# Mean, variance and 1e-6 of the solu by scales of powers of two, and four one-column operations off the vector engine

## The chip, the cores and the metric

The kernel runs on one core of one Trainium2 chip. The metric is the device time of one execution in microseconds (us), lower is better. The core's engines, with the names that the profile uses, are TensorE (PE; PEld is its weight load), VectorE (DVE), ScalarE (ACT), GpSimd (POOL) and SyncE (SP, which here only issues transfers). Each works through its own queue in order, and they wait for each other by semaphores.

## The reference

Attention over chunks of 64 positions, then a feed-forward layer whose activation is a "solu" with a layer norm. The inputs are 8 batches, 8 heads, 576 positions and 64 columns a head, so 4608 tokens of 512 columns; the hidden layer has 1024 columns. The weights `w_in` and `w_out` come in 64-bit floats, the output is 32-bit.

```python
scores = scale * np.matmul(q_c, k_c.transpose(0, 1, 2, 4, 3))
scores = scores - np.max(scores, axis=-1, keepdims=True)
attn = np.exp(scores)
attn = attn / (np.sum(attn, axis=-1, keepdims=True) + 1e-09)
out = np.matmul(attn, v_c)
...
h = x @ w_in
e = np.exp(h - np.max(h, axis=-1, keepdims=True))
sm = e / (np.sum(e, axis=-1, keepdims=True) + 1e-09)
solu = h * sm
mu = np.mean(solu, axis=-1, keepdims=True)
var = np.mean((solu - mu) ** 2, axis=-1, keepdims=True)
ln = (solu - mu) / np.sqrt(var + 1e-06) * g_ln
return (ln @ w_out).astype(np.float32)
```

The division by the sum of exponentials cancels in the layer norm, up to 1e-6: with s that sum, the kernel leaves `h * e` undivided and adds 1e-6 times (s + 1e-9) squared to the variance.

## The kernel before

The 4608 tokens are 36 tiles of 128, numbered from 0. For each tile the kernel makes the scores and the softmax of two chunks (`sx` in PSUM, `s_e` or `e` beside it), turns the weights round into `attn_t`, multiplies with `v` into `x`, splits `x` into a high and a low part (`x_h`, `x_l`), and computes `ph = x @ w_in` as 24 products of 128x128 by 128x512: high times low, high times high, low times high. There is one `ph` buffer, so a tile's sums start only when the tile before has been read out of it. The solu follows, then the transposed `z` is split into `z_h` and `z_l`, and 24 products with `wo_h` and `wo_l` make `po`, in three thirds; `store` scales by `r` and writes out.

What the solu does to a tile, and on which engine:

- `solu_a`: VectorE takes the maximum of `ph` (`h_nmax`), ScalarE the exponential (`z`, with its row sum `h_sum`).
- `solu_b`: VectorE multiplies `ph` by it in place (`z`, row sum `z_sum`) and makes `nmean`, minus the mean, one column. Then the mean is subtracted, on GpSimd for tiles 0 to 4 and on ScalarE from tile 5 on.
- `solu_c`: VectorE adds 1e-9 to the sum (`ssum`), and makes 1e-6 times its square (`eps`), both one column.
- `variance`: ScalarE sums the squares (`sq`, `ssq`), VectorE makes `u = ssq / 1024 + eps`, one column, and GpSimd `r = u ** -0.5`.

The program has two parts. The opening is the table `START`: loads, the conversion of the 64-bit weights into a high and a low 32-bit part (16 pieces, `w_a`, `w_p2`, `w_r`, mostly VectorE and GpSimd), and the first five tiles. There a scheduler decides the order of the instructions on each engine, so that a removed instruction can move others. From tile 5 on (`order.on`) every engine keeps the order in which the loop at the end of the function issues.

GpSimd and SyncE share the transfers that finish the transposes: 8 of 16 for `z_t` and 4 of 8 for `attn_t` go out by each, every second tile.

Of the kernel before, what the change touches and what calls it, by code (L numbers as in the profile page):

```python
# [50 lines left out]
def chunk_attention_then_solu_ffn(  # L51
# [20 lines left out]
    NCC = DM // P  # L72
    NFC = FF // P
    SCALE = 1.0 / float(D) ** 0.5
    LO_DVE = (0, 6, 7, 10, 14)
    LO_TT = (0, 1, 3, 5, 6, 8)
    LO_POOL = (0, 1, 3, 4, 5)
# [10 lines left out]
    const = ctx.enter_context(tc.tile_pool(name="const", bufs=1))  # L88
    stage = ctx.enter_context(tc.tile_pool(name="stage", bufs=2))
    work = ctx.enter_context(tc.tile_pool(name="work", bufs=2))  # L90
    small = ctx.enter_context(tc.tile_pool(name="small", bufs=3))
# [5 lines left out]
    order = Order(tc)  # L97
    order.on = False
    pe, dve, act, pool, sync = (
        order.engine(e)  # L100
        for e in (nc.tensor, nc.vector, nc.scalar, nc.gpsimd, nc.sync)
    )
# [2 lines left out]
    make_identity(nc, ident)  # L105
    mhalf = const.tile([P, 1], F32, name="mhalf")
    nc.gpsimd.memset(mhalf, -0.5)
    g_sb = const.tile([P, NFC], F32, name="g_sb")
    ident_r = const.tile([P, P], F32R, name="ident_r")
    nc.vector.tensor_copy(out=ident_r, in_=ident)  # L110
# [2 lines left out]
        out=minus_r, in0=ident, scalar1=-1.0, scalar2=None, op0=ALU.mult  # L113
# [108 lines left out]
    def piece_rest(x):  # L222
# [30 lines left out]
        pe.matmul(ps, one_r, r, start=False, stop=True)  # L253
        if x in LO_DVE:
            dve.tensor_copy(out=d, in_=ps)
# [47 lines left out]
    def chunk_of(i, c):  # L303
        n = 2 * i + c
        return n // NCH, n % NCH

    def qk_turn(i):

        (b0, n0), (b1, n1) = chunk_of(i, 0), chunk_of(i, 1)
        if b0 == b1:  # L310
            parts = [(b0, n0, 0, 2)]
        else:
            parts = [(b0, n0, 0, 1), (b1, n1, 1, 2)]
        qk_tiles(i)
        for b, n, c0, c1 in parts:
            g = slice(2 * n, 2 * n + 2 * (c1 - c0))
            for to, of in ((QT, QS), (KT, KS)):
                dve.transpose(
                    out=to[i][:, :, c0 * CH:c1 * CH],
                    in_=of[b][:, :, g, :].rearrange("p a g d -> p a (g d)"),  # L320
                )
# [19 lines left out]
    def load_v(i):  # L341
        V[i] = work.tile([P, H, D], F32, name="v_sb", bufs=4)
        for p0, p1, b, s in tile_parts(i):
            sync.dma_start(
                V[i][p0:p1], v[b, :, s:s + p1 - p0, :].rearrange("h t d -> t h d")
            )
# [15 lines left out]
    st = {}  # L362
# [22 lines left out]
    def softmax_a(i):  # L385
# [12 lines left out]
        )  # L398
        act.activation(e, e, AF.Exp, scale=SCALE)
        st[i, "e"] = e  # L400
# [88 lines left out]
    def ffn_in(i):  # L489
        xh, xl = st[i, "x"]  # L490
        ph = st[i, "h"] = ps_h.tile([P, 2, HALF], F32, name="ph")

        sums = [(n, cc, m) for n in range(2) for cc in range(NCC) for m in range(3)]
        if i == 0:
            sums.sort(key=lambda s: s[1])
        else:

            sums.sort(key=lambda s: (s[0], s[2] == 2))
        for n, cc, m in sums:
            cols = slice(n * HALF, (n + 1) * HALF)  # L500
            x, w = ((xh, wi_l), (xh, wi_h), (xl, wi_h))[m]
            pe.matmul(
                ph[:, n, :], x[:, cc, :], w[:, cc, cols],
                start=(cc == 0 and m == 0), stop=(cc == NCC - 1 and m == 2),
            )
# [12 lines left out]
    def solu_b(i):  # L518
        ph = st.pop((i, "h")).rearrange("p n f -> p (n f)")
        z, esum = st.pop((i, "he"))  # L520
        zsum = small.tile([P, 1], F32, name="z_sum")
        dve.scalar_tensor_tensor(
            out=z, in0=ph, scalar=1.0, in1=z, op0=ALU.mult, op1=ALU.mult,
            accum_out=zsum,
        )
        nmean = small.tile([P, 1], F32, name="nmean")
        dve.tensor_scalar(
            out=nmean, in0=zsum, scalar1=-1.0 / FF, scalar2=None, op0=ALU.mult
        )
        if order.on:  # L530
            act.activation(z, z, AF.Identity, bias=nmean)
        else:
            pool.tensor_scalar(
                out=z, in0=z, scalar1=1.0, scalar2=nmean, op0=ALU.mult, op1=ALU.add
            )
        st[i, "z"] = z, esum
        if not order.on:
            solu_c(i)

    def solu_c(i):  # L540
        z, esum = st[i, "z"]

        ssum = small.tile([P, 1], F32, name="ssum")
        dve.tensor_scalar(
            out=ssum, in0=esum, scalar1=1e-9, scalar2=None, op0=ALU.add
        )
        eps = small.tile([P, 1], F32, name="eps")
        dve.scalar_tensor_tensor(
            out=eps, in0=ssum, scalar=1e-6, in1=ssum, op0=ALU.mult, op1=ALU.mult
        )  # L550
        st[i, "z"] = (z, eps)

    def variance(i):
        z, eps = st.pop((i, "z"))
        sq = work.tile([P, FF], mybir.dt.bfloat16, name="sq", bufs=1)
        ssq = small.tile([P, 1], F32, name="ssq")
        act.activation(sq, z, AF.Square, accum_out=ssq)
        u = small.tile([P, 1], F32, name="u")
        dve.scalar_tensor_tensor(
            out=u, in0=ssq, scalar=1.0 / FF, in1=eps, op0=ALU.mult, op1=ALU.add  # L560
        )
        r = small.tile([P, 1], F32, name="r", bufs=7)
        pool.tensor_tensor(out=r, in0=u, in1=mhalf, op=ALU.pow)
        st[i, "n"] = (z, r)
# [5 lines left out]
    def z_turn(i):  # L570
        z, _ = st[i, "n"]
        if i % 2 == 0:
            turned["b"] = work.tile([P, 4, 2, NFC, 32], F32, name="z_b", bufs=1)
        zb = turned["b"]
        dve.transpose(
            out=zb[:, :, i % 2, :, :].rearrange("p q a t -> p a q t"),
            in_=z.rearrange("p (a q c) -> p a q c", q=4, c=32),
        )
        alone = direct(i + 1)
        if i % 2 == 1 or alone:  # L580
            zt = work.tile([P, 4, 2, NFC, 32], F32, name="z_t")
            of = slice(0, 1 if alone else 2)
            for x in range(4):
                for y in range(4):
                    (pool if (x + y) % 2 else sync).dma_start(
                        zt[x * 32:(x + 1) * 32, y, of].rearrange("p s a t -> p (s a t)"),
                        zb[y * 32:(y + 1) * 32, x, of].rearrange("p s a t -> p (s a t)"),
                    )
            for m in (i,) if alone else (i - 1, i):
                st[m, "zr"] = zt  # L590
# [4 lines left out]
    def z_split(i, f):  # L595
        zt = st[i, "zr"][:, :, i % 2, :, :].rearrange("p y a t -> p a y t")
        zhv, zlv = (x.rearrange("p a (y t) -> p a y t", t=32) for x in (ZH, ZL))
        act.copy(zhv[:, f], zt[:, f])
        dve.tensor_tensor(
            out=zlv[:, f], in0=zt[:, f], in1=zhv[:, f].bitcast(F32), op=ALU.subtract  # L600
        )
# [59 lines left out]

    def load_g():
        nc.sync.dma_start(g_sb, g_ln.rearrange("(a p) -> p a", p=P))

    loads = []

    def load_some(n):
        for f, *args in loads[:n]:
            f(*args)
        del loads[:n]  # L670

    def load_batch(b):
        loads.extend(qk_loads(b))


    def direct(m):
        return m < 2 or m == NT - 1
# [43 lines left out]
    for i in range(first, NT):  # L721
        order.on = i >= ORD

        if i + 3 < NT and next_batch < B and chunk_of(i + 3, 0)[0] == next_batch - 1:
            load_batch(next_batch)
            next_batch += 1
        if i + 3 < NT:
            load_v(i + 3)
            qk_turn(i + 3)
        if not direct(i - 1):  # L730
            z_turn(i - 1)
        z_split(queue[0][0], slice(0, NFC))
        ahead = i == NT - 1
        load_some(4 if i % 2 == 0 else 6)
        ffn_in(i)

        if i + 3 < NT:
            scores(i + 3)
        if i + 1 < NT:
            values(i + 1)  # L740
        solu_a(i)

        def part():
            if ahead:
                third_ahead()
            else:
                third()

        part()
        if i + 3 < NT:  # L750
            softmax_a(i + 3)
        if i + 1 < NT:
            x_high(i + 1)
        solu_b(i)
        if i + 3 < NT:
            softmax_b(i + 3)
            attn_turn(i + 3)
        load_some(3 if i % 2 == 0 else 5)
        if i + 1 < NT:
            x_low(i + 1)  # L760
        solu_c(i)
        part()
        variance(i)
        part()
    while queue:
# [33 lines left out]
```

## Time and profile before

| | us |
|---|---|
| median of 3 runs | 517.52 (516.67 to 517.53) |
| the profiled execution | 519.47 |
| its span, first to last instruction | 517.7 |
| TensorE busy | 485.9, 94% of the span |
| mean granted TensorE clock | 0.98 |
| chain that ended last, by engine | PE 82%, DVE 8%, DMA 3%, ACT 2% |

The span of the profile is cut below into stretches: to about 120 us the opening, then the loop, from about 505 us the last tile. In the rows of a timeline the first number is the start in us from the span's start, the second the duration; in square brackets stands how long the engine was idle before, and what released it. In the rows of groups the numbers behind the bar are the busy time in us, the mean of one in ns, and the idle time before. In the rows of waits they are the total in us, how often, and the longest. An instruction on VectorE starts a little before the one ahead of it has ended, so what it costs a full queue is the distance between two starts.

### The profile page before, as it was taken

What the parts mean: (1) busy time and instruction counts of PE and PEld (TensorE: products, weight loads), DVE (VectorE), ACT (ScalarE), POOL (GpSimd) and SP (SyncE); (2) the same over time, 40 slices, a digit from 0 to 9 for tenths busy, and PEclk for the clock granted to TensorE, in tenths of its full rate; (3) what the DMA queues carried; (4) which work ended last, traced back from release to release, by engine and by line L of the source; (5) the groups of instructions that cost most, each with busy time, mean ns of one, the idle gap of its engine ahead of it and who ended that gap; (6) DMA issues with size and microseconds to landing.
All of it is one profiled execution on the core that took longest, in us unless ns stands there. A gap on an engine that the chain in (4) does not pass through costs nothing.

```text
span 517.7 us, 11241 instructions
## 1 busy us (share of the span) xinstructions
PE 485.9 (94%) x4190; PEld 388.7 (75%) x4190; DVE 408.5 (79%) x714; ACT 268.3 (52%) x412; POOL 170.2 (33%) x291
## 2 busy tenths in 40 slices
PE   3779879989999999999999999999899999999997
PEld 2355657768887888888888888888688888887876
DVE  5999976777888888888888888888678888874531
ACT  4858764534444455555555555454355554444452
POOL 4774742540413223131313131413231405043300
PEclk9988979989999999999999999999899999999999
DMA  9996794530777566767576448675747434352211
GB/s 272 347 234 149 127 161 75 126 103 22 170 148 172 133 152 140 169 163 152 145 160 153 108 125 163 158 167 147 141 128 157 120 106 126 80 144 73 79 47 48
DMA packets 204454, 72.33 MB, mean 140 GB/s; under 512 B 188592, under 2 KB 189104, under 8 KB 204016
## 3 DMA queue, kind: packets, MB, share of 16 engines
q1 hardware_dynamic: 192800, 49.58, 43.9%
q0 software_dynamic: 6272, 12.60, 9.4%
q10 hardware_dynamic: 5328, 9.44, 4.9%
q8 instruction: 33, 0.54, 0.4%
q14 instruction: 21, 0.17, 0.1%
HBM read 36.97 MB, written 9.44 MB: 90 GB/s over the span
## 4 chain that ended last, share of the span: by engine, by line
PE 82%; DVE 8%; DMA 3%; ACT 2%; issue 2%; SPq 1%; POOL 0%; ACTq 0%; DVEq 0%
PE po L42 39%; PE ph L42 35%; PE sx L42 7%; DVE w_a L42 4%; DMA attn_t<-a_b 2%; PE tp L42 1%; SPq L42 1%; DMA nat<-in_k_dram 1%; DVE w_p L42 1%; DVE h_nmax L42 1%; ACT z L42 1%; DVE z L42 0%; DMA q_st<-in_q_dram 0%; DVE s_sum L42 0%; ACT o_sb L42 0%
## 5 line engine op out<-in xcount | busy, mean ns | idle before, releaser
L42 PE MATMUL ph<-wi_l,x_h 128*128 128x512 f32 x288 | 114.8, 399 | 8.5 <-ACT w_r L42 3.6
L42 PE MATMUL po<-wo_l,z_h 128*128 128x512 f32 (+1 forms) x288 | 115.9, 402 | 0.3 <-ACT z_h L42 0.3
L42 PE MATMUL ph<-wi_h,x_h 128*128 128x512 f32 x288 | 114.4, 397 | 0.0
L42 PE MATMUL po<-wo_h,z_l 128*128 128x512 f32 (+1 forms) x288 | 112.4, 390 | 0.0
L42 PE MATMUL po<-wo_h,z_h 128*128 128x512 f32 (+1 forms) x288 | 112.3, 390 | 0.0
L42 ACT ACTIVATE z<-ph,h_nmax 128x1024 f32<-128x1024 f32 x36 | 40.2, 1116 | 138.6 <-DVE h_nmax L42 138.6
L42 DVE TENSOR_REDUCE h_nmax<-ph 128x1 f32<-128x1024 f32 x36 | 44.0, 1223 | 48.7 <-PE ph L42 48.6
L42 POOL DMA_DIRECT2D z_t<-z_b x136 | 67.6, 505 | 36.3 <-DVE z_b L42 32.0
L42 PE MATMUL ph<-wi_h,x_l 128*128 128x512 f32 x288 | 78.5, 391 | 0.7 <-DVE x_l L42 0.7
L42 POOL TENSOR_TENSOR r<-u,mhalf 128x1 f32<-128x1 f32 x36 | 20.5, 569 | 175.7 <-DVE u L42 165.1
L42 PEld LDWEIGHTS ph<-wi_l,x_h 128*128 128x128 f32 x288 | 55.3, 192 | 21.5 <-ACT wo_l L42 4.0
L42 PEld LDWEIGHTS po<-wo_l,z_h 128*128 128x128 f32 x288 | 54.5, 189 | 12.8 <-ACT z_h L42 0.7
L42 PEld LDWEIGHTS ph<-wi_h,x_h 128*128 128x128 f32 x288 | 55.3, 192 | 11.5
L42 PEld LDWEIGHTS ph<-wi_h,x_l 128*128 128x128 f32 x288 | 54.3, 189 | 12.8 <-DVE x_l L42 1.4
L42 PEld LDWEIGHTS po<-wo_h,z_l 128*128 128x128 f32 x288 | 54.4, 189 | 11.9 <-DVE z_l L42 0.4
L42 PEld LDWEIGHTS po<-wo_h,z_h 128*128 128x128 f32 x288 | 54.6, 189 | 10.0
L42 POOL DMA_DIRECT2D attn_t<-a_b x60 | 29.5, 498 | 73.3 <-PE po L42 64.3
L42 DVE SCALAR_TENSOR_TENSOR z<-ph,z 128x1024 f32<-128x1024 f32 x36 | 43.9, 1219 | 5.7 <-ACT z L42 5.5
L42 ACT CAST z_h<-z_t 128x1024 fp32r<-128x1024 f32 (+1 forms) x35 | 35.1, 1002 | 23.7 <-DMA attn_t<-a_b 13.5
L42 DVE TENSOR_TENSOR z_l<-z_t,z_h 128x1024 fp32r<-128x1024 f32 (+1 forms) x35 | 39.6, 1132 | 8.7 <-ACT z_h L42 8.7
L42 DVE STREAM_TRANSPOSE z_b<-z 128x1024 f32<-128x1024 f32 x33 | 39.9, 1210 | 2.6 <-POOL z L42 1.3
L42 ACT ACTIVATE z<-z,nmean 128x1024 f32<-128x1024 f32 x31 | 35.7, 1153 | 10.1 <-DVE nmean L42 10.1
(97 smaller groups left out, 676.0 us busy)
## 6 DMA issues: line engine op xcount, KB each, us to landing
out_dram<-o_sb ACTq DMA_DIRECT2D x35, 256.0 KB, 3.1
v_sb<-in_v_dram SPq DMA_DIRECT2D x32, 256.0 KB, 3.7
z_t<-z_b SPq DMA_DIRECT2D x128, 64.0 KB, 2.8
z_t<-z_b POOLq DMA_DIRECT2D x128, 64.0 KB, 2.5
q_st<-in_q_dram SPq DMA_DIRECT2D x112, 72.0 KB, 2.5
k_st<-in_k_dram SPq DMA_DIRECT2D x112, 72.0 KB, 2.5
w_raw<-in_moe_w_out_dram SPq DMA_DIRECT2D x4, 1024.0 KB, 9.6
attn_t<-a_b SPq DMA_DIRECT2D x60, 64.0 KB, 2.3
```

Of the source, the lines that this page charges most:

```text
L42: ins = make(*args, **kwargs)
```

## The change

The product is taken with -1, so that its row sum `z_sum` is minus the sum. Instead of subtracting the mean, the next step computes -1024 times the negative product plus `z_sum`, which is 1024 times the centred value; `nmean` is no longer made. The square is taken of that times 1/(1024 x 32), so its sum is the variance itself, and `u` is a plain sum, now on GpSimd. `eps` is one ScalarE operation, the square of 1e-3 times the sum of exponentials plus 1e-12. The factor 1024 is taken out of `g_sb`, once, on GpSimd. All factors but 1e-3 and 1e-12 are powers of two. `solu_c` is gone: `ssum` and `eps` no longer run on VectorE, `eps` is made in `variance`.

```diff
+    tiny = const.tile([P, 1], F32, name="tiny")
+    nc.gpsimd.memset(tiny, 1e-12)
...
         dve.scalar_tensor_tensor(
-            out=z, in0=ph, scalar=1.0, in1=z, op0=ALU.mult, op1=ALU.mult,
+            out=z, in0=ph, scalar=-1.0, in1=z, op0=ALU.mult, op1=ALU.mult,
             accum_out=zsum,
         )
-        nmean = small.tile([P, 1], F32, name="nmean")
-        dve.tensor_scalar(
-            out=nmean, in0=zsum, scalar1=-1.0 / FF, scalar2=None, op0=ALU.mult
-        )
         if order.on:
-            act.activation(z, z, AF.Identity, bias=nmean)
+            act.activation(z, z, AF.Identity, scale=-float(FF), bias=zsum)
         else:
             pool.tensor_scalar(
-                out=z, in0=z, scalar1=1.0, scalar2=nmean, op0=ALU.mult, op1=ALU.add
+                out=z, in0=z, scalar1=-float(FF), scalar2=zsum, op0=ALU.mult, op1=ALU.add
             )
...
-        ssum = small.tile([P, 1], F32, name="ssum")
-        dve.tensor_scalar(
-            out=ssum, in0=esum, scalar1=1e-9, scalar2=None, op0=ALU.add
-        )
         eps = small.tile([P, 1], F32, name="eps")
-        dve.scalar_tensor_tensor(
-            out=eps, in0=ssum, scalar=1e-6, in1=ssum, op0=ALU.mult, op1=ALU.mult
-        )
+        act.activation(eps, esum, AF.Square, scale=1e-3, bias=tiny)
...
-        act.activation(sq, z, AF.Square, accum_out=ssq)
+        act.activation(sq, z, AF.Square, scale=1.0 / (FF * 32), accum_out=ssq)
         u = small.tile([P, 1], F32, name="u")
-        dve.scalar_tensor_tensor(
-            out=u, in0=ssq, scalar=1.0 / FF, in1=eps, op0=ALU.mult, op1=ALU.add
-        )
+        pool.tensor_tensor(out=u, in0=ssq, in1=eps, op=ALU.add)
...
         nc.sync.dma_start(g_sb, g_ln.rearrange("(a p) -> p a", p=P))
+        nc.gpsimd.tensor_scalar(
+            out=g_sb, in0=g_sb, scalar1=1.0 / FF, scalar2=0.0, op0=ALU.mult, op1=ALU.add
+        )
```

The change also moves instructions, since the scheduler orders the opening anew. Three places follow.

VectorE in the opening, from the maximum of tile 1's `ph` (`h_nmax_686`, after the change `h_nmax_685`) to the product of tile 1 (`z_688`, after the change `z_687`) and on. A number behind a name tells the copies of a buffer apart. First before, then after:

```order
L42 TENSOR_REDUCE h_nmax_686<-ph_653 128x1
L42 TENSOR_SCALAR w_p2_868<-w_a_727 128x512
L42 TENSOR_SCALAR w_a_861<-w_a_861 128x512
L42 TENSOR_SCALAR s_sum_705<-s_sum_705 128x8
L42 SCALAR_TENSOR_TENSOR w_a_861<-w_raw_489,w_a_861 128x512
L42 RECIPROCAL s_rinv_708<-s_sum_705 128x8
L42 SCALAR_TENSOR_TENSOR z_688,z_sum_761<-ph_653,z_688 128x1024
L42 TENSOR_SCALAR ssum_766<-h_sum_689 128x1
L42 TENSOR_SCALAR w_p2_1018<-w_a_861 128x512
L42 TENSOR_TENSOR x_l_650<-sx_98,x_h_649 128x512
L42 STREAM_TRANSPOSE qT_810<-q_st_560 128x512
```

```order
L42 TENSOR_REDUCE h_nmax_685<-ph_652 128x1
L42 TENSOR_SCALAR w_p2_855<-w_a_726 128x512
L42 TENSOR_SCALAR w_a_848<-w_a_848 128x512
L42 TENSOR_SCALAR s_sum_704<-s_sum_704 128x8
L42 SCALAR_TENSOR_TENSOR w_a_848<-w_raw_492,w_a_848 128x512
L42 RECIPROCAL s_rinv_707<-s_sum_704 128x8
L42 STREAM_TRANSPOSE qT_803<-q_st_557 128x512
L42 TENSOR_SCALAR w_p2_1007<-w_a_848 128x512
L42 SCALAR_TENSOR_TENSOR z_687,z_sum_760<-ph_652,z_687 128x1024
L42 TENSOR_TENSOR x_l_649<-sx_100,x_h_648 128x512
```

The transpose `qT` and one `w_p2` stood behind the product and now stand ahead of it. Ahead of `h_nmax` the queue holds the same instructions as before, but for tile 0's `ssum`, `nmean`, `eps` and `u`, which are gone.

ScalarE in the opening, around the exponential of tile 3 (`z_1101`, after the change `z_1092`) and the first output tile (`o_sb`). First before, then after:

```order
L42 ACTIVATE s_e_928<-s_e_928 128x512
L42 ACTIVATE z_1101,h_sum_1102<-ph_1052,h_nmax_1099 128x1024
L42 ACTIVATE o_sb_1089<-po_987,r_631 128x512
L650 DMA out_0_dram<-o_sb_1089 128x512
L42 CAST x_h_966<-sx_98 128x512
```

```order
L42 ACTIVATE s_e_917<-s_e_917 128x512
L42 ACTIVATE o_sb_1080<-po_976,r_630 128x512
L636 DMA out_0_dram<-o_sb_1080 128x512
L42 ACTIVATE z_1092,h_sum_1093<-ph_1043,h_nmax_1090 128x1024
L42 ACTIVATE eps_1153<-h_sum_1093,tiny_86 128x1
L42 CAST x_h_955<-sx_100 128x512
```

The first output tile and its store now come ahead of the exponential. On TensorE, the products of the first output tile that lie between tile 3's sums and the next scores are three instead of six; the other three moved ahead of tile 3's sums.

VectorE in the loop, one tile, behind the softmax of the tile three ahead. First before, then after:

```order
L42 STREAM_TRANSPOSE a_b<-e_100 128x8x2x32
L42 TENSOR_TENSOR x_l<-sx,x_h 128x512
L42 TENSOR_SCALAR ssum<-h_sum 128x1
L42 SCALAR_TENSOR_TENSOR eps<-ssum 128x1
L42 SCALAR_TENSOR_TENSOR u<-ssq,eps 128x1
L42 STREAM_TRANSPOSE qT<-q_st 128x512
```

```order
L42 STREAM_TRANSPOSE a_b<-e_101 128x8x2x32
L42 TENSOR_TENSOR x_l<-sx,x_h 128x512
L42 STREAM_TRANSPOSE qT<-q_st 128x512
L42 STREAM_TRANSPOSE kT<-k_st 128x512
L42 STREAM_TRANSPOSE z_b<-z 128x8x4x32
```

Three of the four are gone here, and `nmean` further up; nothing else moves in the loop. ScalarE has `eps` between the subtraction and the square, GpSimd `u` ahead of each `r`.

More of the change, by code (lines that the diff above doesn't have):

```diff
@@ L74, in chunk_attention_then_solu_ffn @@
     SCALE = 1.0 / float(D) ** 0.5
+    assert FF == 32 * 32
     LO_DVE = (0, 6, 7, 10, 14)
@@ L522, in solu_b, with variance @@
         dve.scalar_tensor_tensor(
-            out=z, in0=ph, scalar=1.0, in1=z, op0=ALU.mult, op1=ALU.mult,
+            out=z, in0=ph, scalar=-1.0, in1=z, op0=ALU.mult, op1=ALU.mult,
             accum_out=zsum,
         )
-        nmean = small.tile([P, 1], F32, name="nmean")
-        dve.tensor_scalar(
-            out=nmean, in0=zsum, scalar1=-1.0 / FF, scalar2=None, op0=ALU.mult
-        )
         if order.on:
-            act.activation(z, z, AF.Identity, bias=nmean)
+            act.activation(z, z, AF.Identity, scale=-float(FF), bias=zsum)
         else:
             pool.tensor_scalar(
-                out=z, in0=z, scalar1=1.0, scalar2=nmean, op0=ALU.mult, op1=ALU.add
+                out=z, in0=z, scalar1=-float(FF), scalar2=zsum, op0=ALU.mult, op1=ALU.add
             )
         st[i, "z"] = z, esum
[L537 to L541, printed above, removed]
-        ssum = small.tile([P, 1], F32, name="ssum")
-        dve.tensor_scalar(
-            out=ssum, in0=esum, scalar1=1e-9, scalar2=None, op0=ALU.add
-        )
-        eps = small.tile([P, 1], F32, name="eps")
-        dve.scalar_tensor_tensor(
-            out=eps, in0=ssum, scalar=1e-6, in1=ssum, op0=ALU.mult, op1=ALU.mult
-        )
-        st[i, "z"] = (z, eps)
-    def variance(i):
-        z, eps = st.pop((i, "z"))
+    def variance(i):
+        z, esum = st.pop((i, "z"))
+        eps = small.tile([P, 1], F32, name="eps")
+        act.activation(eps, esum, AF.Square, scale=1e-3, bias=tiny)
         sq = work.tile([P, FF], mybir.dt.bfloat16, name="sq", bufs=1)
         ssq = small.tile([P, 1], F32, name="ssq")
-        act.activation(sq, z, AF.Square, accum_out=ssq)
+        act.activation(sq, z, AF.Square, scale=1.0 / (FF * 32), accum_out=ssq)
         u = small.tile([P, 1], F32, name="u")
-        dve.scalar_tensor_tensor(
-            out=u, in0=ssq, scalar=1.0 / FF, in1=eps, op0=ALU.mult, op1=ALU.add
-        )
+        pool.tensor_tensor(out=u, in0=ssq, in1=eps, op=ALU.add)
         r = small.tile([P, 1], F32, name="r", bufs=7)
@@ L760, in chunk_attention_then_solu_ffn @@
             x_low(i + 1)
-        solu_c(i)
         part()
```

## The prediction

> **What bounds the kernel now.** I read the page's busy times first, then busy time by stretch, then who TensorE waits for, and last the two stretches that the change re-orders, instruction by instruction.
>
> ```profile
> PE 485.9 (94%) x4190; PEld 388.7 (75%) x4190; DVE 408.5 (79%) x714; ACT 268.3 (52%) x412; POOL 170.2 (33%) x291
> ```
> ```profile
> 20.00:40.00 20.00, 13.22 (x112) 8.65 (x111) 19.55 (x30) 13.63 (x27) 14.53 (x14) 0.91 0.97 273
> 40.00:60.00 20.00, 17.62 (x153) 12.23 (x154) 20.00 (x39) 17.22 (x34) 12.08 (x13) 0.92 0.73 139
> 60.00:68.20 8.20, 4.59 (x51) 3.11 (x51) 8.20 (x16) 4.47 (x10) 5.08 (x7) 0.94 0.80 138
> 68.20:96.00 27.80, 27.19 (x258) 21.10 (x258) 18.94 (x40) 13.96 (x29) 8.86 (x9) 0.89 0.53 91
> 96.00:120.00 24.00, 21.68 (x205) 17.17 (x205) 16.93 (x30) 9.35 (x18) 11.63 (x18) 0.93 0.46 119
> 120.00:360.00 240.00, 240.00 (x2158) 196.15 (x2157) 205.55 (x361) 126.03 (x179) 67.88 (x135) 1.00 0.64 146
> 360.00:380.00 20.00, 18.18 (x131) 14.76 (x130) 13.96 (x22) 7.44 (x11) 5.63 (x12) 0.91 0.66 150
> 380.00:505.00 125.00, 124.45 (x1008) 100.93 (x1007) 90.28 (x157) 62.81 (x90) 34.65 (x69) 1.00 0.40 105
> ```
>
> The rows give start:end, length, then busy time of PE, PEld, DVE, ACT and POOL, then the granted clock. The average of 79% for VectorE hides two regimes. From 120 to 360 us TensorE is busy all 240 of 240 us, and again nearly all of the time to 505: nothing taken from VectorE there can shorten the run, only re-timed work that makes TensorE wait can lengthen it. From 20 to 68 us VectorE is the full engine (19.55, 20.00 and 8.20 us of each stretch) and TensorE idles. So the result is decided in the opening, and there the order of VectorE's queue counts for more than 0.15 us operations.
>
> **The steady loop: nothing, or less than a tenth of a microsecond.** Per tile VectorE loses four operations, ScalarE gets `eps` (128x1) between the subtraction and the square, and GpSimd gets `u` ahead of `r`.
>
> ```profile
> 347.15 0.69 ACT L42 ACTIVATE o_sb<-po,r 128x512 f32<-128x512 f32 x1 [0.62 <-PE po L42]
> ```
> ```profile
> L42 POOL TENSOR_TENSOR r<-u,mhalf 128x1 f32<-128x1 f32 x36 | 20.5, 569 | 175.7 <-DVE u L42 165.1 <-DMA k_st<-in_k_dram 10.4
> ```
> ```profile
> L42 ACT ACTIVATE o_sb<-po,r 128x256 f32<-128x256 f32 x1 | 0.5, 474 | 3.7 <-PE po L42 3.7
> ```
>
> No row shows a one-column activation. It lies between nothing and the 0.474 us of a 256-column one; I take 0.2 us. Behind it on ScalarE stand the square and `o_sb`, which waits 0.62 us for TensorE anyway, so even the upper end is covered; without that cover the 0.2 to 0.47 us would fall on `o_sb` and the next `z_h`. On GpSimd `u` lies between nothing and the 0.569 us of `r`; the engine waits 165 us for `u` over the run, `r` is used three tiles later, and the transfers queued behind it (8 for `z_t`) wait for VectorE's transpose. So it costs nothing here. 36 times four operations are gone from VectorE, but TensorE waits for none of them.
>
> One stall in the loop has to be placed, since it is 1.8 us of idle TensorE and a slow stretch behind it.
>
> ```profile
> 362.24 1.96 POOL L42 DMA_DIRECT2D attn_t<-a_b  x4 [7.76 <-issue]
> ```
> ```profile
> 461.22 1.96 POOL L42 DMA_DIRECT2D attn_t<-a_b  x4 [4.88 <-PE po L42]
> ```
> ```profile
> q0 software_dynamic: 4096, 8.40, 9.1%
> ```
>
> The first two rows are the same transfer in two tiles, after 7.76 and 4.88 us of idleness. The third counts GpSimd's queue from 0 to 360 us: exactly 4096 packets go before the late one. The changed kernel issues the same transfers on that queue in the same order, so I expect the stall at the same transfer, not removed.
>
> **The end.**
>
> ```profile
> 494.49 0.15 DVE L42 TENSOR_SCALAR nmean<-z_sum 128x1 f32<-128x1 f32 x1
> ```
> ```profile
> 496.38 0.50 PE L42 MATMUL po<-wo_l,z_h 128*128 128x512 f32 x1 [0.26 <-ACT z_h L42]
> ```
>
> For the last tile the subtraction waits for `nmean`, then `z_h`, then TensorE (0.26 us). Without `nmean` this chain is 0.1 to 0.15 us shorter: **-0.1 us**.
>
> **The opening, first term: VectorE up to tile 1's product.** TensorE's sums for tile 2 write the single `ph` buffer, so they start when VectorE has multiplied tile 1's `ph` into `z`.
>
> ```profile
> 66.89 1.17 DVE L42 SCALAR_TENSOR_TENSOR z<-ph,z 128x1024 f32<-128x1024 f32 x1
> ...
> 68.05 0.42 DVE L42 TENSOR_SCALAR w_p<-w_a 128x512 uint32<-128x512 uint32 x1
> 68.38 0.69 DVE L42 TENSOR_TENSOR x_l<-sx,x_h 128x512 fp32r<-128x512 f32 x1
> 68.98 0.70 DVE L42 STREAM_TRANSPOSE qT<-q_st 128x512 f32<-128x512 f32 x1
> ```
> ```profile
> 68.21 0.77 PE L42 MATMUL ph<-wi_l,x_h 128*128 128x512 f32 x1 [3.62 <-ACT w_r L42]
> ```
> ```profile
> 56.80 0.14 DVE L42 TENSOR_SCALAR nmean<-z_sum 128x1 f32<-128x1 f32 x1
> ```
> ```profile
> 56.92 0.41 DVE L42 TENSOR_SCALAR w_p<-w_a 128x512 uint32<-128x512 uint32 x1
> ```
>
> The product ends at 66.89 + 1.17 = 68.06 and TensorE starts at 68.21 after 3.62 us of idleness. The row names ScalarE's `w_r`, which ends at the same moment. Ahead of the product the new order has the same VectorE work, less four one-column operations, plus one `w_p2` and one `qT` transpose (the order shown with the change). In a full queue an instruction costs the distance to the next start: 68.38 - 68.05 = 0.33 us for `w_p2`; the 0.69 us `x_l` takes 0.60, so the 0.70 us transpose 0.61. Two one-column operations, 56.80 to 56.92, cost 0.12 together, so four save 0.24 (bounds: 0.24, or four times 0.15 = 0.6, by their durations). Sum: 0.61 + 0.33 - 0.24 = **+0.7 us**. VectorE has no idle time here to hide it in. Bounds: +0.3 by the larger saving, +1.1 if the new queue also waits once more.
>
> **The opening, second term: between tile 3's and tile 4's sums.**
>
> ```profile
> 90.80 1.07 PE L42 MATMUL ph<-wi_h,x_l 128*128 128x512 f32 x4
> ...
> 93.15 0.69 PE L42 MATMUL sx<-kT,qT 64*64 64x64 f32 x32
> ...
> 96.09 0.50 PE L42 MATMUL ph<-wi_l,x_h 128*128 128x512 f32 x1 [0.49 <-ACT x_h L42]
> ```
> ```profile
> 93.22 1.11 ACT L42 ACTIVATE z<-ph,h_nmax 128x1024 f32<-128x1024 f32 x1 [2.68 <-DVE h_nmax L42]
> ...
> 94.33 0.68 ACT L42 ACTIVATE o_sb<-po,r 128x512 f32<-128x512 f32 x1
> 95.03 0.38 ACTq L650 DMA_DIRECT2D out_dram<-o_sb  x1
> 95.45 0.59 ACT L42 CAST x_h<-sx 128x512 fp32r<-128x512 f32 x1 [0.45 <-PE tp L42]
> ```
>
> Tile 3's sums end at 91.87. Six `po` products then fill TensorE to 93.15, 0.21 us each. In the new order three of the six stand earlier, where TensorE is full, so only three fill this gap: 0.64 us of cover is lost. And ScalarE now does `o_sb` and its store before tile 3's exponential. The third `po` ends near 92.55, `o_sb` takes 0.68 and the issue 0.38, so the exponential starts near 93.7, not 93.22. The exponential, the product (1.24 us behind its start, 1.2 long) and the start then come at 96.3, 0.2 us later than 96.09. Together **+0.85 us**; bounds 0.3 (the new order's cover found elsewhere) to 1.3.
>
> The other re-ordered places have cover.
>
> ```profile
> L42 ACT ACTIVATE sq<-z 128x1024 bf16<-128x1024 f32 x36 | 38.1, 1058 | 3.9 <-POOL z L42 2.4 <-POOL s_e L42 0.5
> ```
>
> Tile 3's `x_h` now stands behind tile 2's square on ScalarE; TensorE has the out products of tile 0 and two weight pieces to do in that stretch, so I cost it at nothing; if that cover falls short, the square is the price, 1.06 us by the row above. The scaling of `g_sb` (128x8) stands on GpSimd straight ahead of its first readers there; it lies between nothing and the 0.57 us of `r`, and GpSimd is busy 14.53 of the 20 us around it, so nothing again.
>
> **Sum.** +0.7 + 0.85 - 0.1 = +1.45 us. The profiled execution took 519.47 us (span 517.7), 1.95 above the median of the runs, 517.52. On the profile's time this gives 520.9, on the median 519.0 us, which I forecast.
>
> **The clock, and a rule that I weigh.** After idle stretches the granted clock falls.
>
> ```profile
> PE ph L42 <- ACT x_h L42: 2.7, 2, 2.2
> ```
> ```profile
> PE sx L42 <- DMA attn_t<-a_b: 2.1, 2, 1.8
> ```
>
> The longest of these waits are 2.2 us (at 111 us) and 1.8 us (at 367 us); the stretches around them have clocks of 0.93 and 0.91, that is 24 x 0.07 = 1.7 and 20 x 0.09 = 1.8 us of clock lost. The second term lets TensorE idle some 1.8 us near 94. The Trainium skill, page "TensorE: Matmul & The Clock Gate", section "HAM oscillation — how this bites in real kernels", gives the rule that there should be no idle gaps above about 3.4 us; by it this gap costs nothing more and the sum stays at 519.0. The trace disagrees: its waits of 1.8 and 2.2 us were each followed by a slow stretch, so the price stands below as a rival.
>
> **The rivals.**
> - *One slow stretch more* at the new gap: +1.7, 520.7 us. For it: the two gaps above. Against it: where the stretches fall differs by execution, and one now behind 68 us (clock 0.89 to 96) may shrink.
> - *VectorE's long instructions fall elsewhere* (faster). One place decides, VectorE from 55 to 67 us:
>
> ```profile
> 61.51 1.50 DVE L42 TENSOR_SCALAR w_a<-w_a 128x512 uint32<-128x512 uint32 x1
> ```
>
> The same operation takes 0.41 to 0.42 us elsewhere. Two such stretched rows, 1.1 us each, are 2.2 us; if the new order avoids both, tile 1's product comes 1.5 us earlier rather than 0.7 later and the time is 519.0 - 2.2 = 516.8. From 1.45 us saved on, it is no longer slower. For it: tile 0's product stands earlier in the new queue. Against it: GpSimd's work beside it is the same. The Trainium skill, page "GPSIMD Engine Reference", section "1. Specifications", says that the two engines share their interfaces to SBUF for some VectorE instructions; by that rule GpSimd's new `u` could also stretch one more row, up to 0.57 us.
> - *ScalarE releases tile 2's sums*, as that row says. Its `w_r` stands earlier in the new order; then the first term is gone: 518.3 us, within 0.2%.
> - *The stall at 362 us goes away*: 1.8 us of idleness and 1.8 us of slow clock: 519.0 - 3.6 = 515.4 us. Against it: the equal packet count.
>
> **How the numbers follow.** Forecast 0.40 (its own range 518.2 to 519.8), slow stretch 0.15, VectorE's stretches 0.22, ScalarE 0.15, stall gone 0.08. A measurement of this kernel tells 0.2%, 1.03 us, from no change: below 516.5 or above 518.55. Slower: three quarters of 0.40 and all of 0.15, 0.45. Faster: half of 0.22 and the 0.08, 0.19. Same: the rest, 0.36. The range runs from the middle of the faster case, 516.2, past the slow stretch to 521.2.
>
> **What would show it.** In the new profile: VectorE without `nmean`, `ssum`, `eps`, `u`; TensorE full from 120 to 360; tile 2's sums starting about 0.7 us after 68.2; an idle TensorE of about 1.8 us before tile 4's sums; GpSimd's late transfer again behind 4096 packets. I am wrong if tile 2's sums start before 68, if the loop from 120 on shows new waits, or if the steady distance between tiles changes.

## The result, and the profile after

The changed kernel takes 522.95 us (median of 4 executions, 521.83 to 523.31), the kernel before beside it 517.52: a ratio of 1.0104, 95% interval 1.0083 to 1.0124. It is 1% slower; 519.0 with a range up to 521.2 was forecast. Measured once more in a later job it was 521.70 against 518.14, ratio 1.0079 (1.0049 to 1.0108).

First the page's busy times of the changed kernel, then two of the stretches of the prediction (start:end, length, then PE, PEld, DVE, ACT, POOL busy, then the granted clock).

```profile
PE 489.0 (94%) x4190; PEld 388.9 (75%) x4190; DVE 396.1 (76%) x570; ACT 271.7 (52%) x448; POOL 177.7 (34%) x329
```
```profile
120.00:360.00 240.00, 240.00 (x2216) 195.92 (x2215) 195.00 (x274) 124.21 (x194) 71.82 (x154) 1.00 0.71 145
...
380.00:505.00 125.00, 124.92 (x1012) 101.41 (x1011) 86.65 (x118) 64.11 (x100) 39.27 (x84) 1.00 0.43 108
```

VectorE has 144 instructions and 12.4 us of work less, as the change says, and TensorE is as full in the loop as it was. So the loss must lie ahead of 120 us. One instruction places it: VectorE's product of tile 5, the first tile of the loop. Its row before and after:

```profile
121.40 1.21 DVE L42 SCALAR_TENSOR_TENSOR z<-ph,z 128x1024 f32<-128x1024 f32 x1
```
```profile
125.57 1.21 DVE L42 SCALAR_TENSOR_TENSOR z<-ph,z 128x1024 f32<-128x1024 f32 x1
```

It comes 4.17 us later, and from there to the end of the span are 517.7 - 121.4 = 396.3 us before and 521.5 - 125.57 = 395.9 after. In these two profiles all of the loss is in the opening. (In the profile of the later measurement the product stands at 124.20, 2.8 us later than before, with 395.2 us behind it.) TensorE's timeline of the changed kernel there:

```profile
30.70 2.07 PE L42 MATMUL po<-w_a,ident 128*128 128x512 f32 x2 [0.82 <-DVE w_a L42]
...
42.62 2.08 PE L42 MATMUL po<-w_a,g_diag 128*128 128x512 f32 x2 [4.03 <-DVE w_a L42]
...
56.59 0.47 PE L42 MATMUL ph<-wi_l,x_h 128*128 128x512 f32 x1
...
58.61 0.69 PE L42 MATMUL sx<-kT,qT 64*64 64x64 f32 x32
59.23 1.19 PE L42 MATMUL ph<-wi_h,x_l 128*128 128x512 f32 x4
...
71.29 0.69 PE L42 MATMUL tp<-ident,s_e 128*128 128x128 f32 x2 [4.68 <-POOL s_e L42]
72.81 0.76 PE L42 MATMUL ph<-wi_l,x_h 128*128 128x512 f32 x1 [0.82 <-DVE z L42]
...
100.20 0.47 PE L42 MATMUL ph<-wi_l,x_h 128*128 128x512 f32 x1 [0.57 <-DVE z L42]
```

The same places before:

```profile
30.09 0.50 PE L42 MATMUL ph<-wi_h,x_l 128*128 128x512 f32 x1 [0.71 <-DVE x_l L42]
...
39.98 1.13 PE L42 MATMUL sx<-kT,qT 64*64 64x64 f32 x32 [3.96 <-ACT kT L42]
...
55.42 0.47 PE L42 MATMUL ph<-wi_l,x_h 128*128 128x512 f32 x1 [2.16 <-DVE ssum L42]
```

The waits have changed places. Inside tile 0's sums TensorE now waits for a weight piece (30.70), where before it waited about as long for `x_l` (30.09). It waits for the next piece (42.62), where before it waited for `kT` (39.98). And it waits for the softmax of tile 3 (71.29), where before it waited for tile 1's product (68.21). (Counted from the start, the scores at 39.98 are tile 2's; some of the expectations below name these scores and this softmax a tile too low.) Tile 1's sums start at 56.59, 1.17 us later than before, with the scores of tile 3 now among them (58.61; before, they came ahead of these sums). Tile 2's sums start at 72.81, 4.60 us later, tile 4's at 100.20, 4.11 later. So 3.4 of the 4.6 us arise between 56 and 73 us. VectorE there, between the maximum of tile 1 and its product:

```profile
66.33 1.21 DVE L42 TENSOR_REDUCE h_nmax<-ph 128x1 f32<-128x1024 f32 x1
...
68.24 1.76 DVE L42 SCALAR_TENSOR_TENSOR w_a<-w_raw,w_a 128x512 uint32<-128x512 uint32 x1
...
70.04 0.66 DVE L42 STREAM_TRANSPOSE qT<-q_st 128x512 f32<-128x512 f32 x1
70.62 0.90 DVE L42 TENSOR_SCALAR w_p<-w_a 128x512 uint32<-128x512 uint32 x1
71.44 1.21 DVE L42 SCALAR_TENSOR_TENSOR z<-ph,z 128x1024 f32<-128x1024 f32 x1
```
```profile
64.25 1.21 DVE L42 TENSOR_REDUCE h_nmax<-ph 128x1 f32<-128x1024 f32 x1
```

The last row is before's. The maximum comes 2.08 us later than there, and the product 5.11 us behind it instead of 66.89 - 64.25 = 2.64.

### The profile page after: what moved, and what is told of

The parts are those of the page before. It is cut to its first block, busy times and chain, and to the rows that moved or that the text cites. A ratio compares the mean times of both kernels' runs of the same rounds, so it can differ in the third digit from the quotient of the medians.

```text
span 521.5 us, 11157 instructions
## 1 busy us (share of the span) xinstructions
PE 489.0 (94%) x4190; PEld 388.9 (75%) x4190; DVE 396.1 (76%) x570; ACT 271.7 (52%) x448; POOL 177.7 (34%) x329
## 4 chain that ended last, share of the span: by engine, by line
PE 86%; DVE 4%; DMA 4%; issue 2%; ACT 2%; SPq 1%; POOL 1%; ACTq 0%; POOLq 0%
PE po L42 40%; PE ph L42 37%; PE sx L42 7%; DVE w_a L42 3%; DMA v_sb<-in_v_dram 2%; PE tp L42 2%; DMA attn_t<-a_b 1%; DMA w_raw<-in_moe_w_in_dram 1%; SPq L42 1%; DVE z L42 1%; ACT z L42 0%; DVE w_p L42 0%; ACT o_sb L42 0%; SPq L339 0%; POOL attn_t L42 0%
## 5 line engine op out<-in xcount | busy, mean ns | idle before, releaser
L42 PE MATMUL ph<-wi_h,x_l 128*128 128x512 f32 x288 | 79.9, 396 | 0.0
L42 POOL TENSOR_TENSOR u<-ssq,eps 128x1 f32<-128x1 f32 x36 | 7.2, 201 | 154.2 <-ACT sq L42 153.8
L42 DVE TENSOR_TENSOR z_l<-z_t,z_h 128x1024 fp32r<-128x1024 f32 (+1 forms) x35 | 40.8, 1165 | 24.2 <-ACT z_h L42 23.0
L42 ACT ACTIVATE sq<-z 128x1024 bf16<-128x1024 f32 x36 | 37.6, 1044 | 4.7 <-POOL z L42 4.2
```

The source lines that it names most:

```text
L42: ins = make(*args, **kwargs)
```

## Experiments

A time is the median of its executions, beside it that of the kernel before in the same job; ratios below are to it, with their 95% intervals. They are worked out from all executions and differ a little from the quotient of the two medians.

| run | us (executions) | before | ratio |
|---|---|---|---|
| new_ops_old_order | 516.81 (12) | 518.15 | 0.9975 (0.9956 to 0.9994) |
| old_ops_new_order | 522.87 (6) | 518.15 | 1.0099 (1.0075 to 1.0123) |
| no_g_scale | 516.08 (10) | 518.15 | 0.9961 (0.9946 to 0.9976) |
| late_place_undone | 522.03 (6) | 518.15 | 1.0065 (1.0040 to 1.0091) |
| early_old | 521.62 (12) | 517.70 | 1.0064 (1.0043 to 1.0085) |
| early_new | 519.59 (12) | 517.70 | 1.0032 (1.0009 to 1.0054) |
| product_first | 517.79 (12) | 517.70 | 0.9985 (0.9966 to 1.0004) |
| products_first | 517.30 (12) | 517.70 | 1.0010 (0.9984 to 1.0036) |
| early_place_undone | 521.32 (12) | 517.89 | 1.0065 (1.0045 to 1.0086) |
| late_place_and_word | 520.83 (12) | 517.89 | 1.0058 (1.0029 to 1.0086) |
| products_first_2 | 519.00 (12) | 517.89 | 1.0024 (1.0002 to 1.0046) |
| gaps_filled | 522.18 (6) | 518.14 | 1.0082 (1.0050 to 1.0115) |
| changed_again | 521.70 (6) | 518.14 | 1.0079 (1.0049 to 1.0108) |
| best_filled | 514.87 (12) | 518.14 | 0.9952 (0.9926 to 0.9979) |
| before_and_scaling | 522.68 (6) | 518.72 | 1.0076 (1.0048 to 1.0103) |

**Operations against order.** A kernel can be held to any order: at the end of the function each instruction of an engine is tied behind the one that a table puts ahead of it. The numbers in the table count the engine's instructions as the program issues them.

```diff
+    ORDERS = {"DVE": "0-6 12-15 7 16 8 17-18 9 19 10 20 11 21-27 45 28 46 ...", ...}
+    for name, text in ORDERS.items():
...
+        for a, b in zip(line, line[1:]):
+            tc.add_manual_dep(own[b], own[a].name, no_sync, reason="order")
```

> The operations of the change, but every engine's instructions in the order of the kernel before; what only the change has stands straight ahead of its reader (`eps` ahead of the square, `u` ahead of `r`, the scaling of `g_sb` ahead of its first reader). Theory A, the order of the opening costs it all: the time of before or a little less, 516.8 to 517.8 us, and tile 4's sums start at about 96 us as in before (100.2 in the changed kernel). Theory B, the operations themselves cost it (`eps` on ScalarE, `u` and the scaling on GpSimd): 522 to 523 us in this order too.

> The operations of the kernel before, in the order of the changed kernel; the four one-column operations of a tile stand behind the product, and `u` behind the square. Theory A: 522 to 524 us, with tile 2's sums starting at 72 to 74 us. Theory B: 517 to 518 us.

Both came out as theory A has it: 516.81 and 522.87 us. In the old order the new operations are even 0.25% faster than before; in the new order the old operations lose as much as the change. Tile 5's product in the two profiles, the new operations in the old order first:

```profile
119.84 1.21 DVE L42 SCALAR_TENSOR_TENSOR z<-ph,z 128x1024 f32<-128x1024 f32 x1
```
```profile
125.47 1.21 DVE L42 SCALAR_TENSOR_TENSOR z<-ph,z 128x1024 f32<-128x1024 f32 x1
```

In these profiles the new operations gain 121.40 - 119.84 = 1.56 us in the opening; the new order costs it all and 4 us more. (In the second run the order differs in one place from the changed kernel's: the first transposes of the loop, `qT` and `kT` of tile 8 and `z_b` of tile 4, stand behind tile 4's `u`. The loss is there before that: tile 2's sums start at 73.89.) The ties themselves cost nothing that shows: with them and in its own order, the changed kernel of the run gaps_filled takes 522.18 us, and without them 521.70 beside it.

**Which edit turned the order.** The factor 1024 need not be in `g_sb`: `u` and so `r` can hold it.

```diff
-    nc.gpsimd.memset(tiny, 1e-12)
+    nc.gpsimd.memset(tiny, 1e-12 * FF)
...
-        act.activation(eps, esum, AF.Square, scale=1e-3, bias=tiny)
+        act.activation(eps, esum, AF.Square, scale=1e-3 * FF, bias=tiny)
...
-        act.activation(sq, z, AF.Square, scale=1.0 / (FF * 32), accum_out=ssq)
+        act.activation(sq, z, AF.Square, scale=1.0 / 32, accum_out=ssq)
...
-        nc.gpsimd.tensor_scalar(
-            out=g_sb, in0=g_sb, scalar1=1.0 / FF, scalar2=0.0, op0=ALU.mult, op1=ALU.add
-        )
```

> The changed kernel, but the factor 1024 goes into `u` and so into `r` (the square's scale is 1/32, that of `eps` 1e-3 times 1024) and `g_sb` is not scaled; the scheduler orders the opening anew, and the order is neither that of before nor that of the change. Theory A: any place within some 5 us of before is possible, the loop from 120 us on unchanged, so 515 to 523 us, and the difference to before stands in the start of tile 5's sums (111.4 in before). Theory C, the scaling of `g_sb` on GpSimd is what delays the weights: the time of before, 517 to 518 us.

516.08 us: not theory C's 517 to 518, but the loss is gone with that one instruction, and the change's gain of 0.4% is left. The order tells why: against before, TensorE has to move 10 instructions and VectorE 13 to get this kernel's order, and 57 and 39 to get the change's. The other way round, the scaling alone in the kernel before:

```diff
         nc.sync.dma_start(g_sb, g_ln.rearrange("(a p) -> p a", p=P))
+        nc.gpsimd.tensor_scalar(
+            out=g_sb, in0=g_sb, scalar1=1.0, scalar2=0.0, op0=ALU.mult, op1=ALU.add
+        )
```

> The kernel before with one instruction more: `g_sb` (128x8) is multiplied by 1.0 on GpSimd once it is loaded, and the scheduler orders the opening anew; nothing else of the change is in it. Theory G, this one instruction turns the order and the order costs the time: 521 to 523 us, as with the old operations in the new order (522.87), for an instruction that takes 0.26 us. Theory V, the operations taken from VectorE turn the order: 517 to 518.5 us here.

522.68 us, theory G. One instruction of 0.26 us, with the order that the scheduler makes of it, costs 4 us, without anything else of the change. GpSimd's timeline of this run around it, and then TensorE's:

```profile
21.75 0.26 POOL L664 TENSOR_SCALAR g_sb<-g_sb 128x8 f32<-128x8 f32 x1
23.84 1.28 POOL L42 TENSOR_TENSOR w_r<-w_r,w_p 128x512 fp32r<-128x512 f32 x1 [1.83 <-DVE w_p L42]
25.11 0.54 POOL L42 TENSOR_SCALAR g_diag<-ident,g_sb 128x128 f32<-128x128 f32 x1
```
```profile
42.83 2.07 PE L42 MATMUL po<-w_a,g_diag 128*128 128x512 f32 x2 [4.38 <-DVE w_a L42]
...
70.32 1.12 PE L42 MATMUL tp<-ident,s_e 128*128 128x128 f32 x4 [3.56 <-POOL s_e L42]
71.84 0.77 PE L42 MATMUL ph<-wi_l,x_h 128*128 128x512 f32 x1 [0.40 <-DVE ssum L42]
```

They are the changed kernel's waits at the same places. The first `g_diag` of the kernel before, and of the run with the new operations in the old order:

```profile
21.53 0.53 POOL L42 TENSOR_SCALAR g_diag<-ident,g_sb 128x128 f32<-128x128 f32 x1
```
```profile
21.88 0.54 POOL L42 TENSOR_SCALAR g_diag<-ident,g_sb 128x128 f32<-128x128 f32 x1
```

Behind the scaling the scheduler puts a multiplication of `w_r` ahead of `g_diag`, so it starts at 25.11 instead of 21.53; on the other engines too the opening has another order. In the old order the scaling moves it by 0.35 us, and nothing is lost: the scaling's own time is not the cost.

**Which places of the order.** Five runs cut the new order up. The first two join halves of the two tables:

```diff
-order[engine] = new
+order[engine] = old[:n] + [i for i in new if i not in old[:n]]
```

> The operations of the change. Every engine keeps the order of the kernel before up to the maximum over tile 0's sums (about 50 us), and has the order of the change from there on. Theory A1, the part behind 50 us costs it (TensorE's transposes of `s_e` and VectorE's `qT` and `w_p2` ahead of tile 1's product): 520 to 522 us, tile 1's sums at 55 to 57 us, tile 2's sums 15 to 17 us behind them, as in the changed kernel (16.2; 12.8 in before). Theory A2, the part ahead of 50 us costs it (TensorE's order in tile 0's sums and ahead of tile 1's scores, `kT` behind a `wo_h`): 516.5 to 518 us.

> The other half: the order of the change up to the maximum over tile 0's sums, the order of before behind it, with the operations of the change. Theory A1: 516.5 to 518 us. Theory A2: 520 to 522.5 us. If both halves cost something, both runs lie between, and their losses against the run with the new operations in the old order add up to about 6 us.

Both lie between, the third case of the expectation: against the 0.9975 of the whole old order the two lose 0.0089 and 0.0057, 4.6 and 3.0 us, together 7.5. Neither half is innocent; the cut is not clean, since what one order has ahead of 50 us and the other behind comes early in both mixtures.

```diff
 TensorE
-tp<-ident,s_e x2
 ph<-wi_l,x_h / ph<-wi_h,x_h x8
-tp<-ident,s_e x2
+tp<-ident,s_e x4
 VectorE
+z,z_sum<-ph,z
 qT<-q_st
 w_p<-w_a
-z,z_sum<-ph,z
```

> The changed kernel in its own order but for one place: on VectorE tile 1's product stands ahead of the `qT` transpose and `w_p2` again, and on TensorE the two transposes of `s_e` behind the first eight sums of tile 2. Theory A1, this place is most of the loss: the two rows and the transposes are 1.4 us in the changed kernel's trace, so 521.0 to 521.8 us, tile 2's sums at 71.4 instead of 72.8. Theory A2, the order ahead of it (tile 0's and tile 1's sums, 28 to 56 us) is the loss and something else is late at once: 522.5 to 523 us.

One instruction more, on VectorE:

```diff
-w_a<-w_raw,w_a
 s_rinv<-s_sum
 z,z_sum<-ph,z
+w_a<-w_raw,w_a
```

> The run with the late place undone, and one more instruction of VectorE put behind tile 1's product: the `w_a` combination that took 1.76 us beside GpSimd's multiplication (0.69 us elsewhere). Its queue ahead of the product is then that of before, less the combination. If the stretched instruction on the path is the rest of the late loss: tile 1's product 2.6 to 2.9 us behind its maximum (5.1 in the changed kernel, 2.6 in before, 3.7 with only the late place undone), and 520.5 to 521.5 us. If another instruction stretches in its place: as with the late place alone, 522 us.

And the early places alone:

```diff
 TensorE
 ph<-wi_l,x_h / ph<-wi_h,x_h
-po<-w_a,ident / po<-wi_h,minus_r
...
+po<-w_a,ident / po<-wi_h,minus_r
 ph<-wi_l,x_h
...
+sx<-kT,qT x16
 po<-w_a,g_diag
-sx<-kT,qT x16
 ScalarE
 wo_h<-w_a,g_sb
+kT<-tp
+attn_t<-tp x4
 w_a<-w_raw
 wo_h<-w_a,g_sb
-kT<-tp
-attn_t<-tp x4
```

> The changed kernel in its own order but for the places between 28 and 45 us: TensorE does one weight piece behind tile 0's sums up to their fifth pair, not inside them, and tile 1's scores ahead of the next weight piece; ScalarE copies `kT` and `attn_t` ahead of two `wo_h`. If these places carry the early half (the two runs with half an order lost 3.0 and 4.6 us against the new operations in the old order): 519.5 to 521 us. If they only shift idle time, because VectorE's queue is full behind them: 522 to 523 us.

All three lie between the changed kernel and before: 1.0065, 1.0058 and 1.0065, against 1.0104 and 1.0079 of the changed kernel. Each seems to win back 1 to 2 us, but by the second measurement of the change none is told apart from it. With the word behind the product too, product and maximum of tile 1 are 68.24 - 65.35 = 2.89 us apart in that run's profile instead of 5.11, as expected; that profile is of its fastest execution, 517.57 us, and the median still is 520.83. No single place carries the loss.

**Waits or clock.** The granted clock is lower with the new order: 0.974 to 0.980 in the ten executions of the changed kernel, 0.987 in the median of before beside it.

```diff
+    def keep_busy(count, half):
+        for x in range(count):
+            pe.matmul(
+                sx[:, x % 2, half].rearrange("p a k -> p (a k)"),
+                ident_r, wi_h[:, 0, :HP * CH], start=True, stop=True,
+            )
...
-V:0 S:2
+V:0 D:24:1 S:2
...
+        if i == 2:
+            keep_busy(20, 0)
```

> The changed kernel in its own order, with 44 products of 128x128 by 128x256 that nothing reads, written to a part of `sx` that is free there: 24 on TensorE ahead of the weight piece that it waits 4.0 us for at 38 us, 20 ahead of the `s_e` transposes that it waits 4.7 us for at 66 us. No wait gets shorter by them. Theory D, half of the loss is slow clock behind idle windows: no slow stretch behind 42 and 69 us, a mean granted clock of 0.983 to 0.99 instead of 0.975, 518.5 to 521 us. Theory W, only the waits count: 522 to 523.5 us, whatever the clock.

> The changed kernel once more, on the same chip as the run with filled gaps: 522 to 523.5 us and a mean granted clock of 0.974 to 0.98 by both theories.

Filling raised the clock and did not lower the time. The stretch of the first gap, in the changed kernel and in the run with filled gaps:

```profile
38.00:43.00 5.00, 0.97 (x7) 0.73 (x6) 4.97 (x9) 2.28 (x4) 0.94 (x1) 0.87 1.15 274
```
```profile
38.00:43.00 5.00, 4.01 (x35) 3.73 (x32) 4.93 (x9) 1.98 (x4) 1.24 (x1) 1.00 1.16 272
```

TensorE is busy 4.01 us instead of 0.97 there, the clock stays at 1.00 instead of falling to 0.87, and the mean clock of five of the six executions is 0.984 or 0.987. (The profile is of the sixth, 0.977, where a slow stretch still follows the second gap.) The time, 522.18 us, is that of the changed kernel beside it, 521.70, and the executions of the two cover the same range. So the 2 us that theory D gives the clock do not show. A smaller gain is not excluded. Tile 5's sums in the run with filled gaps, and in the changed kernel beside it:

```profile
114.55 0.80 PE L42 MATMUL ph<-wi_l,x_h 128*128 128x512 f32 x1 [2.23 <-ACT x_h L42]
```
```profile
115.79 0.51 PE L42 MATMUL ph<-wi_l,x_h 128*128 128x512 f32 x1 [2.23 <-ACT x_h L42]
```

They start 1.2 us earlier with the filling, and this execution loses it again in slow stretches behind 114 us (its tile 5 product stands at 124.33, the other's at 124.20).

**A better kernel.** Three runs tried to order VectorE by hand, from the kernel without the scaling: the products that release TensorE first, the weight conversion behind them. The first of them on VectorE:

```diff
 w_a<-w_raw,w_a
+h_nmax<-ph
+s_sum<-s_e / s_sum<-s_sum / s_rinv<-s_sum
+z,z_sum<-ph,z
+x_l<-sx,x_h
 wo_l<-w_a,g_sb,wo_h
-s_sum<-s_e
 w_p<-w_a
-h_nmax<-ph
-s_sum<-s_sum
 w_a<-w_a
-s_rinv<-s_sum
 w_a<-w_raw,w_a
-z,z_sum<-ph,z
 w_p<-w_a
 qT<-q_st
-x_l<-sx,x_h
```

> The kernel without the scaling of `g_sb`, in its own order but for VectorE around tile 1: the maximum over tile 1's sums, the softmax sums of tile 2 and tile 1's product stand ahead of the weight conversion (`wo_l`, `w_p2`, two `w_a`). If VectorE's queue ahead of the product sets the start of tile 2's sums, these start some 1.8 us earlier (68.4 us in that kernel's trace), and the time is 514 to 515 us. If the weights or the softmax are late instead, 516 us or more.

> The same with tile 0 too: its maximum behind the softmax sum of tile 1, its exponential ahead of `kT` on ScalarE, its product ahead of the weight conversion; tile 1's exponential ahead of a `wo_h`. Tile 1's sums then start when TensorE is free, at about 54.3 us instead of 56.1, tile 2's at about 64.5 instead of 68.4; if the weights are not late, 512 to 514 us; if the postponed conversion is late for the first output products (from 72 us on), 515 us or more.

> The run with both products first gained nothing, since TensorE waited 4.18 us for a `wo_l` piece that stands in its queue ahead of tile 2's sums and that VectorE now makes later. Here that piece, and the transposes of `s_e`, stand behind the first eight sums of tile 2 on TensorE, and VectorE multiplies tile 1's product ahead of the softmax sums. Tile 2's sums then start at about 66 us instead of 70.1, and the time is 512.5 to 515 us. If TensorE then waits for the postponed weights in another place, 516 us or more.

All three missed: 517.79, 517.30 and 519.00 us, no better than before. By their ratios, 0.9985, 1.0010 and 1.0024 against 0.9961, they are no better than the kernel they started from either, the last two clearly worse. TensorE's next wait in each:

```profile
69.21 0.50 PE L42 MATMUL po<-wo_l,ident_r 128*128 128x512 f32 x1 [2.82 <-DVE wo_l L42]
```
```profile
68.64 0.50 PE L42 MATMUL po<-wo_l,ident_r 128*128 128x512 f32 x1 [4.18 <-DVE wo_l L42]
```
```profile
65.98 0.47 PE L42 MATMUL ph<-wi_l,x_h 128*128 128x512 f32 x1 [0.89 <-DVE z L42]
...
69.94 0.63 PE L42 MATMUL tp<-ident,s_e 128*128 128x128 f32 x4 [1.88 <-issue]
```

First the postponed weight piece is late; in the third run tile 2's sums do start at 65.98 as expected, and the next wait is behind them. In a full queue an instruction put ahead puts another back.

> The kernel without the scaling of `g_sb`, in its own order, with 42 such products in its three gaps: 16 ahead of tile 1's scores (2.43 us of waiting), 12 ahead of tile 1's sums (2.16), 14 ahead of the `s_e` transposes of tile 2 (2.55). Theory D: the slow stretches behind 41 and 68 us go, 513 to 515 us. Theory W: 516 us, as without them.

514.87 us, the fastest of all, 0.48% (0.21 to 0.74) under before; its ratio of 0.9952 is not told apart from the 0.9961 without the filling. What beats both kernels is to leave the scaling of `g_sb` away.

## Why the prediction was wrong

- **What bounds the kernel: right.** The loop is untouched (240.00 of 240 us busy, 395.9 against 396.3 us behind tile 5's product), the opening decides, and the order of VectorE's queue counts for more there than 0.15 us operations. That the change is slower was right too.
- **First term, +0.7: the step that failed.** It is to be the wait ahead of tile 2's sums, and these start 4.60 us later. The sum counted what stands in VectorE's queue ahead of tile 1's product, found it equal but for two instructions, and took the queue for full ("no idle time here to hide it in"). In the profiles the product comes 71.44 - 66.89 = 4.55 us later. Of it 1.40 (70.04 to 71.44) are the two instructions, priced at 0.94; 1.07 is a `w_a` combination of 1.76 instead of 0.69 us, in the changed kernel beside a multiplication on GpSimd, the rival of the stretched rows with the other sign; and 2.08 is that the maximum of tile 1 came later, which was priced at nothing. The sums that it reads do not place it: in both profiles it starts 3.1 us after their end, straight behind other work of the queue. VectorE up to that maximum, before and after (the third busy time is VectorE's), and its two longest waits after 40 us in the changed kernel:

```profile
0.00:64.25 64.25, 44.58 (x368) 29.89 (x368) 57.52 (x96) 42.59 (x78) 40.19 (x48) 0.95 0.87 226
0.00:66.33 66.33, 48.65 (x368) 31.40 (x368) 57.84 (x91) 42.63 (x79) 40.82 (x51) 0.90 0.90 220
```
```profile
44.73 0.29 DVE L42 TENSOR_SCALAR g_diag<-ident,g_sb 128x128 f32<-128x128 f32 x1 [0.56 <-PE po L42]
...
54.46 1.22 DVE L42 SCALAR_TENSOR_TENSOR z<-ph,z 128x1024 f32<-128x1024 f32 x1 [0.55 <-ACT z L42]
```

  VectorE is busy 0.32 us longer, and idle 66.33 - 57.84 = 8.49 us instead of 64.25 - 57.52 = 6.73, 1.76 more. In the new order it waits for TensorE's weight pieces and for tile 0's exponential; before, it has no idle time from 40 us on. An equal set of instructions ahead on VectorE is not an equal time: the new order on TensorE and ScalarE between 28 and 56 us makes VectorE wait, and that was not priced.
- **The scaling of `g_sb`, "so nothing again".** It was priced by its duration and by GpSimd's idle time, and for the instruction that is right (nothing in the old order). But it stands ahead of the first readers in a part that a scheduler orders, and alone it turns that order (522.68 us in the kernel before). The prediction had the turned order before it and priced three places of it.
- **Second term, +0.85: about right as idle time, but a shorter slow stretch covered it.** From tile 2's to tile 4's sums, before and after:

```profile
68.21:96.09 27.88, 27.19 (x259) 21.09 (x259) 18.95 (x41) 14.04 (x29) 8.88 (x10) 0.89 0.53 91
72.81:100.20 27.39, 25.77 (x257) 19.90 (x257) 17.80 (x29) 12.92 (x27) 7.38 (x10) 0.94 0.59 92
```

  TensorE is idle 27.39 - 25.77 = 1.62 us instead of 0.69, 0.93 more (some 1.8 was the sign to look for). But the clock there is 0.94 instead of 0.89, and the stretch takes 0.49 us less, so that tile 4's sums are 4.11 us late where tile 2's were 4.60. That the slow stretch there may shrink stood in the prediction, without a size.
- **ScalarE as releaser of tile 2's sums:** not so; the row at 72.81 names tile 1's product.
- **ScalarE's one-column operation** was put at 0.2 us, between nothing and 0.474. Its group in the changed kernel, and that of `u` on GpSimd (put below 0.569):

```profile
L42 ACT ACTIVATE eps<-h_sum,tiny 128x1 f32<-128x1 f32 x36 | 10.1, 281 | 0.1
...
L42 POOL TENSOR_TENSOR u<-ssq,eps 128x1 f32<-128x1 f32 x36 | 7.2, 201 | 154.2 <-ACT sq L42 153.8
```

  Both lie inside their bounds and behind other work, as expected.
- **The end, -0.1:** within the 0.4 us by which the spans behind tile 5's product differ, so not told apart.
- **The gain of the change itself** was seen only at the end and as 0.24 us in the first term. With the order held it is 0.25% (0.06 to 0.44), 1.3 us, in the opening.
- **Median against profile:** before was profiled in an execution of 519.47 us, 1.95 above its median; the change in one of 523.3, 0.35 above. The profiles differ by 3.8 us, the medians by 5.4.
- **The stall at 362 us** stayed, behind the same packets, as expected (row below).

What stays open: which instruction of the new order causes which of these waits. The halves and the three places say several, and the places do not add up beyond the noise.

## What to carry to other kernels

Where a scheduler orders part of a program, an edit there is two changes, one of work and one of order. Price them apart, by holding the order while the work changes and the other way round; here the work was worth -1.3 us and the order 5 to 7. Where a constant can ride in an operation that exists, as the factor does in `eps` and the square, put it there rather than into an instruction of its own ahead of many readers. And moving work within a full queue gained nothing here: after three hand-made orders TensorE waited elsewhere.

## What the runs showed of the hardware

TensorE's clock does not need a long gap to fall. It is granted in windows of 3.41 us, on a grid that begins elsewhere in each profile. Over the 17 profiles, cut on that grid from about 16 us on: of windows at full clock in which TensorE was busy under 1.5 us, 34 of 34 were followed by one at half clock; from 1.5 to under 2.2 us 27 of 73; from 2.2 us on none of 2164. Four windows of the kernel before, in pairs (busy TensorE first behind the length, the clock third from the end):

```profile
36.53:39.94 3.41, 0.00 (x0) 0.00 (x0) 3.38 (x6) 1.21 (x3) 1.62 (x2) 1.00 1.15 247
39.94:43.36 3.42, 3.38 (x36) 2.08 (x37) 3.42 (x7) 3.25 (x7) 0.00 (x0) 0.50 1.03 284
53.60:57.01 3.41, 1.59 (x7) 1.38 (x8) 3.41 (x10) 3.33 (x8) 1.03 (x3) 1.00 0.85 137
57.01:60.43 3.42, 3.42 (x17) 2.84 (x16) 3.42 (x5) 3.08 (x6) 3.30 (x3) 1.00 0.84 136
```

Nothing in the window at 36.53, and the next is at 0.50; 1.59 us in the window at 53.60, and the next stays at 1.00. So a wait of 2 us lowers the clock where it fills most of one window, and not where the grid cuts it in two. The Trainium skill, page "TensorE: Matmul & The Clock Gate", section "HAM oscillation — how this bites in real kernels", speaks of idle gaps above 3.4 us; here gaps of 1.8 and 2.2 us did it, so the measurement decides. In the kernel without the scaling it cost little: with its three gaps filled (best_filled, clock 0.987 to 1.00) the time fell by no more than the noise.

The stall at 362 us is at 366 in the changed kernel, and again exactly 4096 packets of GpSimd's queue come ahead of it:

```profile
366.12 1.97 POOL L42 DMA_DIRECT2D attn_t<-a_b  x4 [8.58 <-issue]
```
```profile
q0 software_dynamic: 4096, 8.40, 9.3%
```
